# Last scatter behind the branch, three steps' sums and the first turned rows on VectorE, one gather earlier

## The chip, the cores and the metric

The kernel runs on one core of one Trainium2 chip. The metric is the device time of one execution in microseconds; the lower, the better. The core has five engines: PE (TensorE: matrix products), ACT (ScalarE), DVE (VectorE), POOL (GpSimd) and SP (SyncE, which here only issues DMAs). Each engine goes through its own instructions in order; semaphores hold an engine until another engine or a DMA is done. POOL issues the indirect DMAs (gathers and scatters by a list of row numbers).

## The reference

Two blocks follow each other. The first filters each of 8 sequences of 2496 rows and 256 channels in the frequency domain. The second sends each of the 19,968 resulting rows to the best of 8 experts, keeps the 80 rows with the largest gate of each expert, and runs those rows through the expert's two layers; all other rows of the output are zero.

```python
X = np.fft.rfft(x, axis=1)                       # x: 8 x 2496 x 256
y = np.fft.irfft(X * (filt_r + 1j*filt_i)[None], n=2496, axis=1)
x = y.reshape(8*2496, 256)
logits = x @ w_gate                              # 256 x 8
expert_idx = argmax(logits);  gate_w = softmax(logits)[expert_idx]
out = zeros((19968, 256))
for e in range(8):
    tok_idx = the rows with expert_idx == e, the 80 of largest gate_w
    h = np.maximum(x[tok_idx] @ w1[e], 0)        # 256 x 1024
    out[tok_idx] = gate_w[tok_idx, None] * (h @ w2[e])   # 1024 x 256
```

## The kernel before

**Spectra.** A sequence's transform of 2496 = 39 x 64 points is done as products with small tables. A loop over v = 0 to 81 walks through 80 steps (b, u): sequence b, part u of 10. In one turn of the loop stand: `stage2(b, u)`, which multiplies by a table into PSUM (`pb`, L334), takes the products with the filter's real and imaginary part on DVE (two instructions of 128x512, L342) and sums them on POOL (two of 128x256, L348: one subtraction and one addition); `transpose1` and `stage1` for later steps; and `turn` of the step two turns before, which turns the summed tile `p` by a product (`py`, L357), copies the spectrum out with ACT (`z` L372, `ysp` L373) and lets ACT send it to DRAM (`yf`, L376) every second step. SP loads `x` and writes zeros to the output (L193) from `zero_t`, a tile of zeros, at the same time. The order is written out by hand: each engine takes the instructions in the order in which the program gives them out.

**Rows.** Only the rows that an expert keeps are transformed back. From the logits a search finds the rows (`pick_...`, on DVE with small products on PE). For each sequence t, `fetch(t)` gathers the rows' table in two halves of 1280 columns from DRAM into `gts` (POOL, L476; 128 rows of 5 KB a half). `turn_rows(t, g)` turns four blocks of it by PE (`pw`, L493) and copies them to `wt` with ACT (L497); `add_rows(t, g)` multiplies them with four blocks of the sequence's spectrum (`po`, L504). After the fifth group ACT copies the result to `yr` (L509), and SP loads a further spectrum (`yb`, L484) and writes `yr` to `y_sel` in DRAM (L516). The groups of t = 0 to 2 stand in one list, those of t = 3 to 7 in another; `go(n)` gives out the next n entries, and the pieces of the search stand between. `turn_rows(0, 0)` and `turn_rows(0, 1)` stand right behind the last `turn`.

On POOL, the gathers for t = 0 and 1 stand between the last sums of the spectra (turns 76, 77 and 81 of the loop). Those for t = 3 to 5, the products `eval` for the search and the eight gathers of the gates (`gather_gates`, L225: 80 single numbers each) stand in this order:

```python
fetch(NE)              # NE = 3
pick_slots(1)
fetch(NE + 1)
...
pick_slots(2)          # idxs, idxt: the rows' numbers
gather_gates()
fetch(NE + 2)
```

`fetch(6)` and `fetch(7)` follow when the turned rows of t = 3 are given out. POOL's DMAs use eight semaphores in turn, and each waits until the one eight before it has landed.

**Experts.** For each expert the kept rows are gathered from `y_sel` (L1117), turned (`px`, `xs`), multiplied by w1 (`ph`, L1147), passed through relu (`hT`, by ACT and DVE) and multiplied by w2 (`po`, L1162). ACT multiplies by the gate (`ys`, L1165), and POOL scatters the 80 rows to the output (L1167). Expert 7 comes last.

**End.** A rare input (ties, an overfull list) needs a general path. Whether it does, the search has written to `bad`; behind the experts every engine reads this number (L1053) and branches (L1054). The input here doesn't need the path: every engine jumps to a short piece that brings the semaphores to the values which the general path would have left. On POOL this piece waits for all of POOL's DMAs and has an instruction INC_SWDGE_SEM for their semaphores. The program's end (L1566) follows: waits on SP, a DRAIN on POOL, and two barriers.

Of the kernel before, what the change touches and what calls it, by code (L numbers as in the profile page):

```python
# [11 lines left out]
AF = mybir.ActivationFunctionType  # L12
AX = mybir.AxisListType
F32 = mybir.dt.float32
BF16 = mybir.dt.bfloat16
I32 = mybir.dt.int32
# [7 lines left out]
B, S, C = 8, 2496, 256  # L24
N = B * S
N1, N2 = 39, 64
NS, NQ = 20, 64
NU = NS // 2
# [8 lines left out]
E, FF = 8, 1024  # L37
# [44 lines left out]
def kernel(  # L82
# [11 lines left out]
    nc = tc.nc  # L94
# [103 lines left out]

    idxs = consts.tile([cap, E], I32, name="idxs")
    idxg = consts.tile([cap, E], I32, name="idxg")  # L200
    gate = consts.tile([cap, E], F32, name="gate")
    idxt = consts.tile([cap, E], I32, name="idxt")
    idxb = consts.tile([128, B], I32, name="idxb")
# [30 lines left out]
    with ExitStack() as actx:  # L234
# [94 lines left out]
        def stage2(b, u):  # L329
            t2 = st.pop(("t2", b, u))  # L330
            ps = fps.tile([128, NDB, 2, 2, NQ], F32, name=f"pb_{b}_{u}", tag="f")
            for i in range(2):
                for cb in range(NDB):
                    nc.tensor.matmul(  # L334
                        out=ps[:, cb, i], rhs=d_t[:, 2 * u + i, :], start=True, stop=True,
                        lhsT=t2[:, i, 128 * cb:128 * cb + 128])
            pr = []
            for k in range(2):
                pt = ppool.tile([128, 2 * NDB, 2, NQ], F32, name=f"p{k}_{b}_{u}", tag=f"p{k}",
                                bufs=4 - 2 * k)  # L340
                f = ft[k][:, u].rearrange("p c s q -> p (c s) q")
                nc.vector.tensor_tensor(  # L342
                    out=pt, in0=ps[:].rearrange("p c s r q -> p (c s) r q"),
                    in1=f.unsqueeze(2).to_broadcast([128, 2 * NDB, 2, NQ]), op=AL.mult)
                pr.append(pt)
            yt = pr[0]
            for r, op in enumerate((AL.subtract, AL.add)):
                nc.gpsimd.tensor_tensor(out=yt[:, :, r, :], in0=yt[:, :, r, :],  # L348
                                        in1=pr[1][:, :, 1 - r, :], op=op)
            st["yt", b, u] = yt  # L350

        def turn(b, u):
# [136 lines left out]
        def turn_rows(t, g):  # L489
            ps = fps.tile([128, SG, 128], F32, name=f"pw_{t}_{g}", tag="f")  # L490
            for i in range(SG):
                s = SG * g + i
                nc.tensor.transpose(ps[:, i, :], gts[t // 2][:, t % 2, 128 * s:128 * s + 128],  # L493
                                    ident[:])
            if g % 2 == 0:
                wts[t, g // 2] = xpool.tile([128, 2, SG, 128], F32, name=f"wt_{t}_{g}", tag="x")
            nc.scalar.copy(out=wts[t, g // 2][:, g % 2], in_=ps[:])  # L497

        def add_rows(t, g):
            if g == 0:  # L500
# [233 lines left out]
        def pick_slots(part):  # L734
            f_t = st["f_t"]
            if part == 0:
                off_e = pt([128, 1], F32, "off_e", 1)
                nc.vector.tensor_copy(out=off_e[:], in_=st["poff"][:, 2, 0:1])
                slot = pt([128, KR], F32, "slot", 1)
                nc.vector.tensor_scalar(out=slot[:], in0=iota[:, 0:KR], scalar1=off_e[:, 0:1],  # L740
                                        scalar2=None, op0=AL.add)
                st["slot"] = slot
            elif part == 3:
                slot = st["slot"]
                st["eplc"] = xpool.tile([128, KR, cap], BF16, name="eplc", tag="x")
                nc.vector.tensor_tensor(
                    out=st["eplc"][:], in0=slot[:].unsqueeze(2).to_broadcast([128, KR, cap]),
                    in1=iota[:, 0:cap].unsqueeze(1).to_broadcast([128, KR, cap]),
                    op=AL.is_equal)
            elif part == 1:  # L750
                st["eval"] = pt([128, KR, 4, E], BF16, "eval_", 1)
                for i in range(4):
                    nc.gpsimd.tensor_tensor(
                        out=st["eval"][:, :, i, :],
                        in0=f_t[:, i, :].unsqueeze(2).to_broadcast([128, KR, E]),
                        in1=ehot[:].unsqueeze(1).to_broadcast([128, KR, E]), op=AL.mult)
            elif part == 2:
                pe = st["misc"][0:cap, 128:128 + 4 * E]
                for k in range(KR):
                    nc.tensor.matmul(pe, lhsT=st["eplc"][:, k, :],  # L760
                                     rhs=st["eval"][:, k].rearrange("p v e -> p (v e)"),
                                     start=(k == 0), stop=(k == KR - 1))
                es = st["es"] = pt([cap, 4, E], F32, "es", 1)
                nc.vector.tensor_copy(out=es[:].rearrange("p v e -> p (v e)"), in_=pe)
                nc.vector.scalar_tensor_tensor(out=idxg[:], in0=es[:, 1, :], scalar=128.0,
                                               in1=es[:, 0, :], op0=AL.mult, op1=AL.add)
                emp = pt([cap, E], F32, "emp", 1)
                nc.vector.tensor_scalar(out=emp[:], in0=es[:, 3, :], scalar1=st["off"][0:cap, 0:1],
                                        scalar2=float(N + S), op0=AL.is_le, op1=AL.mult)
                tokens(nc, sp, cap, es[:, 1, :], 0.0, es[:, 2, :], es[:, 3, :], -1.0, emp, idxs,  # L770
                       idxt)
            else:
                es = st["es"]
                inl = pt([cap, NO], F32, "inl", 1)
                nc.vector.tensor_scalar(out=inl[:], in0=es[:, 1, 0:NO], scalar1=float(B - 1),
                                        scalar2=None, op0=AL.is_equal)
                nc.vector.scalar_tensor_tensor(out=inl[:], in0=es[:, 0, 0:NO], scalar=1.0,
                                               in1=inl[:], op0=AL.add, op1=AL.mult)
                diag = fp.tile([cap, NO, cap], BF16, name="diag", bufs=1)
                nc.vector.tensor_tensor(  # L780
                    out=diag[:], in0=ident[0:cap, 0:cap].unsqueeze(1).to_broadcast([cap, NO, cap]),
                    in1=inl[:].unsqueeze(2).to_broadcast([cap, NO, cap]), op=AL.mult)
                last = st["last"] = fp.tile([128, NO, cap], F32, name="last", bufs=1)
                pd = st["misc"][:, 192:192 + NO * cap]
                nc.tensor.matmul(pd, lhsT=ones_bf[0:cap, :], start=True, stop=True,
                                 rhs=diag[:].rearrange("p e t -> p (e t)"))
                nc.vector.tensor_scalar(
                    out=last[:].rearrange("p e t -> p (e t)"), in0=pd, scalar1=pid[:, 0:1],
                    scalar2=1.0, op0=AL.subtract, op1=AL.is_equal)

        LATE, LEAD = 2, 2
        with tc.manual_schedule():
# [180 lines left out]
            fetch(NE)  # L973
            pick_slots(1)
            fetch(NE + 1)
            go(FG[5])
            pick_full(1, NE, B)
            pick_bad()
            go(next(i for i, w in enumerate(work) if w[1] == NE))
            pick_slots(2)  # L980
            gather_gates()
            fetch(NE + 2)
            go(8)
            pick_slots(4)
            go(next(i for i, w in enumerate(work) if w[:2] == ("m", B - 1)))
# [16 lines left out]
            for e in range(E):  # L1002
                if e + 3 < E:
                    ex.gather(e + 3)
                if e == 0:
                    ex.layer2(0)
                if e + 1 < E:
                    ex.layer1(e + 1)
                if e + 2 < E:
                    ex.turn(e + 2)  # L1010
                if e > 0:
                    ex.layer2(e)
                if e + 6 < E:
                    weights(e + 6, wpool, "w")

# [38 lines left out]
    with tc.If(n_bad > 0):  # L1054
# [22 lines left out]
        with (  # L1077
# [8 lines left out]
            for e in range(E):  # L1086
                load_weights(e, wp3.tile([128, 2 * NFC * C], F32, name=f"wg_{e}", tag="w"))
                ex.gather(e)
                ex.turn(e)
                ex.layer1(e)  # L1090
                ex.layer2(e)


class Experts:
# [59 lines left out]
                                scalar1=0.0, scalar2=None, op0=AL.max)  # L1154
        self.hT[e] = hT

    def layer2(self, e):
        nc, cap, nm = self.nc, self.cap, self.nm
        hT = self.hT.pop(e)
        po = self.bank(f"po{nm}_{e}")[:, 0:C]  # L1160
        for fc in range(NFC):
            nc.tensor.matmul(po[0:cap, :], lhsT=hT[:, fc, :], rhs=self.w2s[e][:, fc, :],  # L1162
                             start=(fc == 0), stop=(fc == NFC - 1))
        ys = self.fp.tile([cap, C], F32, name=f"ys{nm}_{e}", tag="ys")
        nc.scalar.activation(out=ys[:], in_=po[0:cap, :], func=AF.Copy,  # L1165
                             scale=self.gate[:, e:e + 1])
        nc.gpsimd.indirect_dma_start(  # L1167
            out=self.out[:, :],
            out_offset=bass.IndirectOffsetOnAxis(ap=self.idxs[:, e:e + 1], axis=0),
            in_=ys[:], in_offset=None, bounds_check=N - 1, oob_is_err=False)  # L1170


def tokens(nc, sp, cap, sq, sq0, bf, af, af0, emp, idxs, idxt):
# [397 lines left out]
```

## Time and profile before

| | |
|---|---|
| median of 17 runs | 476.37 us (473.71 to 481.25) |
| the profiled execution's own time | 476.19 us |
| its span, from first to last instruction | 474.4 us |
| mean granted TensorE clock | 0.981 |
| PE, ACT, DVE, POOL busy | 435.3, 222.7, 185.5, 183.8 us |
| DMA | 109.95 MB, 232 GB/s on average |

The span is that of the recorded instructions; the time also has 1.8 us around them. In the rows below, a group is given as line, engine, operation, tile written <- tiles read, partitions x elements, count; the bracket tells how long the engine was idle before it and what ended that. In the view of windows, each stretch has the busy time of PE, PEld (PE's loading of weights), DVE, ACT and POOL, then the granted clock, the DMA engines' share and GB/s. In the view of a line, the three numbers are the shortest, median and longest duration in ns, then the first and last start.

### The profile page before, as it was taken

What the parts mean: (1) busy time and instruction counts of PE and PEld (TensorE: products, weight loads), DVE (VectorE), ACT (ScalarE), POOL (GpSimd) and SP (SyncE); (2) the same over time, 40 slices, a digit from 0 to 9 for tenths busy, and PEclk for the clock granted to TensorE, in tenths of its full rate; (3) what the DMA queues carried; (4) which work ended last, traced back from release to release, by engine and by line L of the source; (5) the groups of instructions that cost most, each with busy time, mean ns of one, the idle gap of its engine ahead of it and who ended that gap; (6) DMA issues with size and microseconds to landing.
All of it is one profiled execution on the core that took longest, in us unless ns stands there. A gap on an engine that the chain in (4) does not pass through costs nothing. (4 is left out here: it accounts for less than half of the span.)

```text
span 474.4 us, 8669 instructions
## 1 busy us (share of the span) xinstructions
PE 435.3 (92%) x3380; PEld 409.9 (86%) x3380; DVE 185.5 (39%) x542; ACT 222.7 (47%) x364; POOL 183.8 (39%) x252
## 2 busy tenths in 40 slices
PE   4979999999999999999999997999939999999970
PEld 4869999999999999999999987888828888888850
DVE  2134554454664455655437984484200000110100
ACT  3846666666766666666667544322212231111110
POOL 7478344443543433543435548204550002113110
PEclk9999999999999999999999999999998999999995
DMA  7998367888777888778961326988857963999010
GB/s 205 264 264 261 127 196 238 244 259 250 262 237 250 270 274 250 208 267 267 386 263 68 121 103 205 356 311 305 310 178 287 368 223 91 376 388 301 8 28 2
DMA packets 39476, 109.95 MB, mean 232 GB/s; under 512 B 5073, under 2 KB 14608, under 8 KB 38658
## 3 DMA queue, kind: packets, MB, share of 16 engines
q1 hardware_dynamic: 28688, 76.41, 49.5%
q10 hardware_dynamic: 6178, 21.04, 11.3%
q0 software_dynamic: 4560, 11.86, 8.0%
q8 instruction: 29, 0.48, 0.4%
q14 instruction: 21, 0.17, 0.1%
HBM read 68.97 MB, written 43.20 MB: 236 GB/s over the span
## 5 line engine op out<-in xcount | busy, mean ns | idle before, releaser
L348 POOL TENSOR_TENSOR p<-p,p 128x256 f32<-128x256 f32 x160 | 114.0, 734 | 136.3 <-DVE p L342 107.9
L342 DVE TENSOR_TENSOR p<-pb,ft 128x512 f32<-128x512 f32 x160 | 102.2, 680 | 17.8 <-PE pb L334 11.3
L315 ACT COPY t<-pa 128x480 f32<-128x480 f32 x88 | 87.0, 1000 | 26.8 <-PE pa L309 26.2
L309 PE MATMUL pa<-wf_t,x 117*128 117x120 f32 x704 | 93.3, 281 | 6.1 <-DMA x<-in_x_dram 5.9
L309 PEld LDWEIGHTS pa<-wf_t,x 117*128 117x128 f32 x704 | 87.5, 198 | 6.2 <-DMA x<-in_x_dram 5.9
L357 PE MATMUL py<-gi,p 128*128 128x136 f32 x640 | 88.1, 280 | 2.3 <-POOL p L348 2.3
L334 PE MATMUL pb<-d_t,t 128*128 128x128 f32 x640 | 85.3, 276 | 2.3 <-remote 2.1
L357 PEld LDWEIGHTS py<-gi,p 128*128 128x128 f32 x640 | 79.8, 190 | 2.9 <-POOL p L348 2.9
L334 PEld LDWEIGHTS pb<-d_t,t 128*128 128x128 f32 x640 | 78.0, 191 | 3.3 <-remote 2.2
L325 ACT COPY t<-pt 128x512 f32<-128x512 f32 x80 | 46.8, 585 | 66.6 <-PE pt L323 60.0
L504 PE MATMUL po<-yb,wt 128*128 128x256 f32 x240 | 58.8, 390 | 8.4 <-ACT wt L497 8.4
L504 PEld LDWEIGHTS po<-yb,wt 128*128 128x128 f32 x240 | 44.7, 196 | 14.3 <-ACT wt L497 9.1
L497 ACT COPY wt<-pw 128x512 f32<-128x512 f32 x40 | 23.1, 586 | 53.4 <-PE pw L493 42.0
L323 PE MATMUL pt<-ident,t 128*128 128x128 f32 x320 | 48.0, 273 | 0.0
L379 DVE COPY z<-py 128x16 f32<-128x16 f32 x60 | 11.2, 186 | 92.0 <-ACT ysp L373 57.9
L323 PEld LDWEIGHTS pt<-ident,t 128*128 128x128 f32 x320 | 37.6, 142 | 0.0
L373 ACT COPY ysp<-py 128x512 f32<-128x512 f32 x60 | 35.4, 590 | 0.0
L1147 PEld LDWEIGHTS ph<-xs,w 128*128 128x128 f32 x256 | 29.7, 192 | 1.7 <-DVE xs L1138 1.1
L1147 PE MATMUL ph<-xs,w 128*128 128x80 f32 x256 | 29.8, 274 | 0.8 <-DVE xs L1138 0.8
L1162 PE MATMUL po<-w,hT 128*80 128x256 f32 x128 | 28.8, 379 | 0.0
L1117 POOL DMA_INDIRECT xg<-y_sel,idxg x8 | 7.7, 962 | 47.5 <-DMA y_sel<-yr 45.6
L1167 POOL DMA_INDIRECT out_dram<-ys,idxs x8 | 7.5, 932 | 46.1 <-ACT ys L1165 46.1
(195 smaller groups left out, 331.8 us busy)
## 6 DMA issues: line engine op xcount, KB each, us to landing
out_dram<-zero_t SPq DMA_DIRECT2D x64, 312.0 KB
x<-in_x_dram SPq DMA_DIRECT2D x40, 468.0 KB
w<-in_moe_w_dram SPq DMA_DIRECT2D x16, 1024.0 KB
yf<-ysp ACTq DMA_DIRECT2D x30, 512.0 KB
yb<-yf SPq DMA_DIRECT2D x6, 2560.0 KB
yf<-ys ACTq DMA_DIRECT2D x10, 512.0 KB
x<-in_x_dram SPq DMA_DIRECT2D x8, 234.0 KB
d_t<-d_tbl SPq DMA_DIRECT2D x5, 256.0 KB
```

Source lines behind the costliest of these rows:

```text
L309: nc.tensor.matmul(out=ps[:, i, :, 2 * NS * cb:2 * NS * cb + 2 * NS], lhsT=xt[0:NJ * N1, (2 * k + i) % JC, 128 * cb:128 * cb + 128], rhs=w ...
L315: nc.scalar.copy(out=t1[:, 2 * k - h:2 * k - h + 2], in_=ps[:])
L323: nc.tensor.transpose(ps[:, i, cb, :], t1[:, a:a + 2, :].rearrange("p r n -> p (r n)"), ident[:])
L325: nc.scalar.copy(out=t2[:].rearrange("p i c -> p (i c)"), in_=ps[:].rearrange("p i c q -> p (i c q)"))
L334: nc.tensor.matmul(out=ps[:, cb, i], rhs=d_t[:, 2 * u + i, :], start=True, stop=True, lhsT=t2[:, i, 128 * cb:128 * cb + 128])
L342: nc.vector.tensor_tensor(out=pt, in0=ps[:].rearrange("p c s r q -> p (c s) r q"), in1=f.unsqueeze(2).to_broadcast([128, 2 * NDB, 2, NQ]), ...
L348: nc.gpsimd.tensor_tensor(out=yt[:, :, r, :], in0=yt[:, :, r, :], in1=pr[1][:, :, 1 - r, :], op=op)
L357: nc.tensor.matmul(out=ps[:, i, ZW * cb:ZW * cb + ZW], rhs=gi[:, cb, :], lhsT=yt[:, 2 * cb + i].rearrange("p r q -> p (r q)"), start=True, ...
L373: nc.scalar.copy(out=dst.rearrange("p s (h w) -> p s h w", h=2), in_=pv[:, :, :, 0:128])
L504: nc.tensor.matmul(pos[t][:, 0, 0:C], lhsT=wts[t, g // 2][:, g % 2, i, :], rhs=ybs[t][:, s, :], start=(s == 0), stop=(s == NS - 1))
L1147: nc.tensor.matmul(ph[:, fc // 4, fc % 4, 0:cap], lhsT=self.w1s[e][:, k, 128 * fc:128 * fc + 128], rhs=xs[:, k, :], start=(k == 0), stop=( ...
L1162: nc.tensor.matmul(po[0:cap, :], lhsT=hT[:, fc, :], rhs=self.w2s[e][:, fc, :], start=(fc == 0), stop=(fc == NFC - 1))
```

## The change

The program changes in four places, and nothing of what is computed does.

1. `stage2`: in the last three steps, (7, 7), (7, 8) and (7, 9), DVE does the two sums of the filter's products; in the others POOL still does.
2. `turn_rows`: DVE copies the first turned rows (t = 0, g = 0); ACT copies the others.
3. `fetch(NE + 2)` stands right behind `fetch(NE + 1)`, ahead of `gather_gates`.
4. Expert 7's result goes into a part of `zero_t` instead of a tile of the pool, and its scatter is given out behind the `if` of the general path, with a copy of its row numbers in a tile of its own (`idx_last`, by DVE). POOL's branch then stands behind the scatter of expert 6. The piece behind the `if` is a new one, from which every engine goes on to the program's end by one more jump.

```diff
+    idx_last = consts.tile([cap, 1], I32, name="idx_last")
+    ys_last = zero_t[0:cap, 0:C]
...
             for r, op in enumerate((AL.subtract, AL.add)):
-                nc.gpsimd.tensor_tensor(out=yt[:, :, r, :], in0=yt[:, :, r, :],
-                                        in1=pr[1][:, :, 1 - r, :], op=op)
+                adder = nc.gpsimd if (b, u) < (B - 1, NU - 3) else nc.vector
+                adder.tensor_tensor(out=yt[:, :, r, :], in0=yt[:, :, r, :],
+                                    in1=pr[1][:, :, 1 - r, :], op=op)
...
-            nc.scalar.copy(out=wts[t, g // 2][:, g % 2], in_=ps[:])
+            copy = nc.vector.tensor_copy if (t, g) == (0, 0) else nc.scalar.copy
+            copy(out=wts[t, g // 2][:, g % 2], in_=ps[:])
...
+                nc.vector.tensor_copy(out=idx_last[:], in_=idxs[:, E - 1:E])
...
             fetch(NE + 1)
+            fetch(NE + 2)
...
             gather_gates()
-            fetch(NE + 2)
...
-                    ex.layer2(e)
+                    ex.layer2(e, keep=ys_last if e == E - 1 else None)
...
+    scatter(nc, out, ys_last, idx_last[:])
...
-    def layer2(self, e):
+    def layer2(self, e, keep=None):
...
-        ys = self.fp.tile([cap, C], F32, name=f"ys{nm}_{e}", tag="ys")
-        nc.scalar.activation(out=ys[:], in_=po[0:cap, :], func=AF.Copy,
+        ys = keep
+        if keep is None:
+            ys = self.fp.tile([cap, C], F32, name=f"ys{nm}_{e}", tag="ys")[:]
+        nc.scalar.activation(out=ys, in_=po[0:cap, :], func=AF.Copy,
                              scale=self.gate[:, e:e + 1])
-        nc.gpsimd.indirect_dma_start(
-            out=self.out[:, :],
-            out_offset=bass.IndirectOffsetOnAxis(ap=self.idxs[:, e:e + 1], axis=0),
-            in_=ys[:], in_offset=None, bounds_check=N - 1, oob_is_err=False)
+        if keep is None:
+            scatter(nc, self.out, ys, self.idxs[:, e:e + 1])
+
+
+def scatter(nc, out, ys, idx):
+    nc.gpsimd.indirect_dma_start(
+        out=out[:, :], out_offset=bass.IndirectOffsetOnAxis(ap=idx, axis=0), in_=ys,
+        in_offset=None, bounds_check=N - 1, oob_is_err=False)
```

## The prediction

> **What bounds the kernel now.** I read the busy shares first, then the windows by stage, then the waits and the timeline where TensorE (PE) has holes, and last the rows behind the final matmul.
>
> ```profile
> PE 435.3 (92%) x3380; PEld 409.9 (86%) x3380; DVE 185.5 (39%) x542; ACT 222.7 (47%) x364; POOL 183.8 (39%) x252
> 340.00:350.00 10.00, 7.23 (x42) 6.21 (x40) 0.47 (x1) 1.17 (x2) 7.76 (x8) 1.00 0.41 132
> 350.00:360.00 10.00, 4.67 (x16) 3.62 (x14) 0.00 (x0) 1.45 (x3) 1.99 (x2) 0.68 0.88 314
> ```
>
> PE is the bound: 435.3 of 474.4 us. A gain must fill one of its holes or shorten the end. There are three: small ones at 292 to 296 us, a large one at 340 to 360 (PE busy 11.9 of 20, granted clock 0.68 in its second half), and 14.9 us behind the last matmul (459.5).
>
> Hole 1, from the timeline:
>
> ```profile
> 290.72 2.77 POOL L348 TENSOR_TENSOR p<-p,p 128x256 f32<-128x256 f32 x4
> 292.19 1.19 PE L357 MATMUL py<-gi,p 128*128 128x136 f32 x8 [1.38 <-POOL p L348]
> 294.57 1.04 PE L493 MATMUL pw<-ident,gts 128*128 128x128 f32 x8
> 295.85 1.07 ACT L497 COPY wt<-pw 128x512 f32<-128x512 f32 x2 [0.40 <-issue]
> 296.49 1.99 PE L504 MATMUL po<-ys,wt 128*128 128x256 f32 x8 [0.88 <-ACT wt L497]
> ```
>
> PE waits 1.38 us for POOL's last sums (1.42 us a step, between gathers of 1.0 us), then 0.88 us for ACT's copy of the turned rows.
>
> Hole 2, from the waits of 294 to 360 us:
>
> ```profile
> PE po L504 <- ACT wt L497: 9.3, 4, 5.3
> ACT yr L509 <- remote: 6.4, 1, 6.4
> ACT wt L497 <- remote: 6.3, 2, 5.9
> ```
>
> PE stood 2.77 us before 347.8 and 5.33 before 355.56, waiting for ACT, and ACT for something the profile can't name ("remote"). It falls into the time in which POOL issues the eight gate gathers (334.9 to 344.7) and six row gathers (345.0 to 352.5). Next the clock halves: the L504 group of 8 at 355.56 took 3.78 us against 1.99, the next groups 0.65 more. Together 2.77 + 5.33 + 1.79 + 0.65 = 10.5 us.
>
> Hole 3, the rows of the branch (L1054) and of the program's end (L1566) after 460 us:
>
> ```profile
> L1054 POOLq EVENT_SEMAPHORE  x5: 17/43/43, 463.4 to 466.2; - x5
> L1054 POOLq COMPARE_BRANCH  x1: 53/53/53, 460.7 to 460.7; - x1
> L1054 POOLq INC_SWDGE_SEM  x1: 1556/1556/1556, 466.3 to 466.3; - x1
> L1566 POOLq DRAIN  x3: 46/103/5623, 467.9 to 474.1; - x3
> L1566 SPq DRAIN  x3: 7/7/13, 468.6 to 473.8; - x3
> ```
>
> POOL alone sets the end: scatter at 460.32, branch at 460.67, first instruction of the path not taken at 463.4 (2.8 us later), the second at 466.0 (a hole of 2.5 us with nothing to wait for), then the 1.56 us INC_SWDGE_SEM and a DRAIN of 5.62 us to 473.5, and 0.85 us of barriers. SP was through at 468.6.
>
> **The change part by part.** All in the times of this execution (476.19 us, span 474.4; the median of the runs is 476.37, so 0.2 above it).
>
> *Sums of the last three steps by VectorE (DVE).* Six additions of 128x256 leave POOL (6 x 0.73 us) and join DVE. No row has just this; L535 (128x256, two SBUF inputs) took 0.42, so a step costs DVE 0.84 more. DVE's products end at 287.35 for the first; with the additions between, the steps end at 288.2, 290.3 and 292.4 (each: products 1.27 + 0.84, PE's pb being there). The last was ready at 293.49 on POOL, so the last turn starts near 292.45 instead of 293.54: -1.1 us. DVE has nothing else but 0.4 us until 301. POOL's four row gathers now follow each other: 287.0, 288.3, 289.6, 290.9 instead of 287.0, 289.7, 293.6, 295.0. They are wanted after 293, so earlier gains nothing itself.
>
> A rule speaks against this. POOL's L348 pair at 281.10 took 2.17 us instead of 1.42 beside two-input DVE work:
>
> ```profile
> 281.10 2.17 POOL L348 TENSOR_TENSOR p<-p,p 128x256 f32<-128x256 f32 x2 [2.77 <-DVE p L342]
> ```
>
> The Trainium skill, "SBUF — State Buffer", section "Who interferes with whom", has it that a DVE instruction with two SBUF inputs and a GpSimd instruction that reads SBUF shut each other out. By the rule each gather may be held by a pair of additions (0.84 us), so the fourth ends 2.5 us later than I say, still before 295. By the row, a 0.75 us stretch at most. The first gather starts before any addition and landed at 292.9, before PE wants it at 293.4. So 0 either way; if that landing slipped past 293.4, the excess would come straight off the 1.1.
>
> *First turned rows by DVE.* ACT at 293 to 295 has z, ysp and a DMA issue ahead of the copies. DVE reads PSUM at 0.29 us for 128x128 (L512) and 0.48 for 128x312 (L406), so 128x512 costs 0.69. Turned rows start at 293.45, their first group ends near 294.0, DVE is through at 294.7, and PE's L504 starts at 294.75 instead of 296.49. ACT's second copy comes at 294.8, while PE wants it 4 us later. Both parts: -1.7 us (0 to -2.2). From there to 342 PE has no hole over 0.9 us, so the lead is kept.
>
> *One gather ahead of the gates.* Two issues (1.0 us each, 1.3 apart) move from behind the eight gate gathers to before them. The gates wait for idxt of DVE in any case (334.9), so their start costs nothing. The eight semaphores of POOL's DMAs go round, so the last two gates now wait for the moved gather to land, in competition with SP's spectrum load (332 to 342). The gates are read only from 408, so 60 us cover this; SP's spectrum, which the moved gather may hold back by 3 us, landed at 342 and is multiplied first after 357. The remaining four row gathers start some 2.6 us earlier. Whether hole 2 shrinks I can't derive, since its cause isn't named. Bounds: nothing left of it (-10.5); longer by the time the moved gather needs in the crowded stretch (1.3 MB at the 0.4 MB/us of 336 to 342: +3.3). I take half of the two issues, -1.3: its second wait ended when the row gathers were through, and there are a third fewer of them.
>
> *Last scatter behind the branch.* POOL no longer waits for the last ys before it branches. The scatter before starts at 456.86, and branch follows 0.35 later: 457.2; path not taken at 460.0. The 2.5 us hole lies at a fixed place of POOL's program (between its 708th and 709th instruction). POOL's program is 11 instructions shorter there, so the hole moves 11 instructions on, right in front of the scatter: INC_SWDGE_SEM runs 460.3 to 461.9 under it, and the scatter starts at 462.7 (its ys is ready at 460.0). It ends at 463.6; then DRAIN 5.62 and barriers 0.85: 470.1 instead of 474.4, so -4.3 us. SP must see the landing (2.1 to 2.7 us after the start by the trace of the last scatter: 465.4) and is through by 466.3, so it is hidden by DRAIN.
>
> What DRAIN waits for no row shows. If it hangs on INC_SWDGE_SEM and lets the scatter pass, the end is 468.5 (-5.9). If it hangs on it and blocks the scatter, 471.9 (-2.5); if it then comes a second time, 475.0 (+0.6). If the hole still lies ahead of INC_SWDGE_SEM, 2.5 us are lost in each. I take -4.3: the row that stands between.
>
> A second rule: each engine gets a further jump to the end. The skill, "Runtime: NRT & Kernel Launch", section "Instruction fetch mechanics", says that a taken branch to code not yet fetched stalls until it is. The taken branch here cost 2.8 us; a second such stall would leave -1.5. But the jump from the path not taken to the end exists already, and DVE went through it from 456.7 to its DRAIN at 456.8: 0.1 us, to neighbouring code. I count nothing.
>
> One DVE copy of idx_last (0.16 us by L1191, with 5 us of slack before L785) and the same ACT write into another tile: 0. The zero writes that read this tile ended long before.
>
> **Sum:** -1.7 - 1.3 - 4.3 = -7.3 us, 468.9 against 476.19, so 469.1 for the median.
>
> **The rivals.**
> *The hole closes* (0.13): fewer gathers behind the gates, no halved clock: -1.7 - 10.5 - 4.3, so 460. For it: the wait ends with the gathers; against: the gates, which may be its cause, stay.
> *The end doesn't gain* (0.22): INC_SWDGE_SEM's work blocks the scatter and hole 2 stays: -1.7 and -2.5 to +0.6, so 472.2 to 475.3.
> *Slower* (0.15): the scatter becomes serial with POOL's closing work. Hole ahead of INC_SWDGE_SEM (464.4), its 5.62 us blocks the scatter until 470.1, then 0.91 and DRAIN again: 477.6, +3.2; with the lead +1.5, 477.9. It decides from a scatter start of 470.1 on (470.1 + 0.91 + 5.62 + 0.85 = 477.5, against 474.4 + 1.7 of lead). For it: the scatter does move behind two steps of unknown cause; against: the branch is taken 3.5 us earlier. A longer hole 2 would end on the same side.
>
> **How the numbers follow.** Main case 0.50: 469.1, own range 466 to 472. About 0.3% (1.4 us) can be told from no change. Faster: 0.50 + 0.13 + most of the 0.22 = 0.77; same 0.09; slower 0.14. The range 461.5 to 477 leaves out half of "closes" and half of "slower".
>
> **What would show it.** Right: last L348 on DVE with PE's first L504 near 294.7; POOL's COMPARE_BRANCH before the last ys; INC_SWDGE_SEM straight after the first event; scatter at 461 (462.7 less the lead) and no row of 2.5 us ahead of it. Wrong: PE's hole at 345 to 355 much shorter or longer; a DRAIN of 5.6 us ahead of the scatter or after it twice; L504 still released by ACT or by the gather.

## The result, and the profile after

The changed kernel takes 463.0 us (median of 8 runs, 461.9 to 465.1) against 476.55 (47 runs): ratio 0.9713, 95% interval 0.9689 to 0.9738, faster by 13.5 us. The profiled executions agree: spans of 460.9 and 474.4 us. The forecast was 469.1. Its direction and its range held; the size did not come from where the sum had it.

The span divides at three points that both traces have: PE's first product with turned rows (`po<-ys`), PE's first product for the experts (`px`), and the end of the last `ys`. Worked out from the starts in the two traces:

| part of the span, us | before | after | difference | forecast |
|---|---|---|---|---|
| start to first `po<-ys` | 296.49 | 294.89 | -1.6 | -1.7 |
| first `po<-ys` to first `px` (rows) | 101.80 | 93.92 | -7.9 | -1.3 |
| first `px` to end of last `ys` (experts) | 61.76 | 61.71 | 0 | 0 |
| end of last `ys` to end of span | 14.34 | 10.35 | -4.0 | -4.3 |

So two of the three terms came out within 0.3 us, and the middle one, which the prediction said it couldn't derive, is six times its size. Executions differ by some 4 us in how soon they come to the last steps of the spectra, whatever the edits. So the front is better counted from PE's third last product into `pb` (284.66 and 284.77 us): from there to the first `po<-ys` it is 11.83 us before and 10.12 after, -1.7; in every run below it is 11.8 without edits 1 and 2 and 10.1 with them.

The front, from the timeline after (start, length, then the instruction group; the bracket is the idle time before it and what ended it):

```profile
291.12 0.99 POOL L479 DMA_INDIRECT gts<-rows_tbl,idxb  x1 [0.31 <-issue]
291.51 0.76 DVE L351 TENSOR_TENSOR p<-p,p 128x256 f32<-128x256 f32 x2
292.42 1.16 PE L360 MATMUL py<-gi,p 128*128 128x136 f32 x8 [0.58 <-issue]
293.42 1.04 PE L496 MATMUL pw<-ident,gts 128*128 128x128 f32 x8
294.06 0.69 DVE L501 COPY wt<-pw 128x512 f32<-128x512 f32 x1 [1.65 <-PE pw L496]
294.89 1.97 PE L508 MATMUL po<-ys,wt 128*128 128x256 f32 x8 [0.44 <-DVE wt L501]
```

A pair of sums takes DVE 0.76 us (0.84 had been worked out), the first turned rows 0.69 (0.69), and PE waits 0.58 and 0.44 us where it waited 1.38 and 0.88.

The middle, from the windows after (columns as in the prediction: PE, PEld, DVE, ACT, POOL, then clock, DMA share, GB/s), with the three rows of the timeline that explain the first window:

```profile
330.00:340.00 10.00, 8.32 (x52) 6.96 (x51) 2.58 (x16) 2.21 (x5) 5.68 (x8) 0.83 0.96 366
340.00:350.00 10.00, 10.00 (x56) 8.72 (x55) 0.47 (x1) 3.13 (x6) 6.40 (x7) 1.00 0.50 180
350.00:360.00 10.00, 10.00 (x57) 8.82 (x57) 0.27 (x1) 3.09 (x6) 1.28 (x2) 1.00 0.90 365
```

```profile
330.17 0.75 PE L764 MATMUL misc<-eval__1_3660,eplc 128*80 128x32 bf16 x16
332.77 0.19 DVE L768 COPY es<-misc 80x32 f32<-80x32 f32 x1 [5.71 <-PE pw L496]
333.52 3.67 PE L508 MATMUL po<-yb,wt 128*128 128x256 f32 x8 [1.68 <-ACT wt L501]
```

PE is busy through 340 to 360, where it was busy for 11.9 of 20 us. A smaller stall is new at 331.8: the product into `misc` ended at 330.9, but DVE's copy of it starts only at 332.8, some 1.8 us late; PE then stands 1.68 us, and the next group of 8 takes 3.67 us instead of 1.99, at half the clock. Idle and slow time together are some 3.5 us, against 10.5 before. The stall before begins in the same way, with a product and ACT's copy of it:

```profile
342.26 0.60 PE L493 MATMUL pw<-ident,gts 128*128 128x128 f32 x4
347.16 0.58 ACT L497 COPY wt<-pw 128x512 f32<-128x512 f32 x1 [5.91 <-remote]
```

The product ends at 342.86 in the record, and the copy follows 4.30 us later, where in e7 below such a copy follows within 0.1 us as a rule and 0.4 at most, if ACT is free. Below, this is called a late semaphore of PE. The ends of PE's records are modelled, so it may also be that the product itself ended later than the record says.

The end, from the rows of the branch (L1059), the last scatter (L1180) and the program's end (L1578): shortest, median and longest duration in ns, then first and last start.

```profile
L1059 POOLq EVENT_SEMAPHORE  x5: 17/43/43, 450.3 to 450.7; - x5
L1059 POOLq COMPARE_BRANCH  x1: 53/53/53, 447.7 to 447.7; - x1
L1059 POOLq INC_SWDGE_SEM  x1: 1540/1540/1540, 450.8 to 450.8; - x1
L1180 POOL DMA_INDIRECT out_dram<-zero_t,idx_last x1: 912/912/912, 453.5 to 453.5; - x1
L1578 POOLq DRAIN  x3: 46/109/6443, 453.6 to 460.6; - x3
```

POOL branches at 447.7, 2.8 us ahead of the end of the last `ys` (450.53). The five events of the path now lie within 0.4 us (2.8 before); the scatter starts at 453.49, and the DRAIN ends at 460.03, 5.63 us behind the scatter's end. There is one DRAIN of this kind, not two.

### The profile page after: what moved, and what is told of

Same layout as the page of the kernel before. It is cut to its first block, busy times and chain, and to the rows that moved or that the text cites. A ratio compares the mean times of both kernels' runs of the same rounds, so it can differ in the third digit from the quotient of the medians.

```text
span 460.9 us, 8667 instructions
## 1 busy us (share of the span) xinstructions
PE 433.8 (94%) x3380; PEld 409.2 (89%) x3380; DVE 188.4 (41%) x550; ACT 222.5 (48%) x363; POOL 179.9 (39%) x246
## 5 line engine op out<-in xcount | busy, mean ns | idle before, releaser
L351 POOL TENSOR_TENSOR p<-p,p 128x256 f32<-128x256 f32 x154 | 110.0, 736 | 136.3 <-DVE p L344 88.8
L344 DVE TENSOR_TENSOR p<-pb,ft 128x512 f32<-128x512 f32 x160 | 102.1, 680 | 17.4 <-PE pb L336 10.9
L311 PE MATMUL pa<-wf_t,x 117*128 117x120 f32 x704 | 92.2, 278 | 7.1 <-DMA x<-in_x_dram 6.9
L311 PEld LDWEIGHTS pa<-wf_t,x 117*128 117x128 f32 x704 | 86.2, 195 | 7.5 <-DMA x<-in_x_dram 6.0
L1168 PEld LDWEIGHTS po<-w,hT 128*80 128x80 f32 x128 | 18.6, 150 | 7.5
L479 POOL DMA_INDIRECT gts<-rows_tbl,idxb x16 | 16.1, 1009 | 21.0 <-DVE idxb L695 16.7
```

What stands on the lines that cost most here:

```text
L311: nc.tensor.matmul(out=ps[:, i, :, 2 * NS * cb:2 * NS * cb + 2 * NS], lhsT=xt[0:NJ * N1, (2 * k + i) % JC, 128 * cb:128 * cb + 128], rhs=w ...
L344: nc.vector.tensor_tensor(out=pt, in0=ps[:].rearrange("p c s r q -> p (c s) r q"), in1=f.unsqueeze(2).to_broadcast([128, 2 * NDB, 2, NQ]), ...
L351: adder.tensor_tensor(out=yt[:, :, r, :], in0=yt[:, :, r, :], in1=pr[1][:, :, 1 - r, :], op=op)
```

## The experiments

Twelve runs were made, each beside the kernel before on the same chip. They fell on four chips, and these differ: on the first (e1 to e4) the kernel before takes 476.3 us, as in the comparison above, on the second (e5 to e8) 465.7, on the third (e9, e10) 466.2 and on the fourth (e11, e12) 466.4. Each ratio is against the kernel before on the same chip. The table has the parts of each profiled execution, as above. The kernel before has a profile on the first chip alone; on the others its time is known, and how it runs there is read from e7, which differs from it by three short instructions.

| kernel | median, us | before there | ratio (95%) | rows | last `ys` to end |
|---|---|---|---|---|---|
| e1 gather only | 467.8 | 476.3 | 0.9821 (0.9797 to 0.9845) | 93.7 | 14.08 |
| e2 gather back | 469.3 | 476.3 | 0.9874 (0.9833 to 0.9916) | 99.0 | 10.65 |
| e3 end only | 475.6 | 476.3 | 0.9971 (0.9941 to 1.0001) | 102.1 | 13.12 |
| e4 front only | 471.4 | 476.3 | 0.9914 (0.9887 to 0.9941) | 100.4 | 12.31 |
| e5 no gates | 460.7 | 465.7 | 0.9881 (0.9845 to 0.9916) | 90.8 | 11.10 |
| e6 gates last | 459.4 | 465.7 | 0.9880 (0.9821 to 0.9939) | 91.1 | 10.74 |
| e7 three more | 463.4 | 465.7 | 0.9947 (0.9915 to 0.9978) | 92.7 | 12.08 |
| e8 gather held | 459.9 | 465.7 | 0.9880 (0.9826 to 0.9933) | 90.8 | 10.72 |
| e9 changed kernel | 459.3 | 466.2 | 0.9834 (0.9785 to 0.9882) | 90.8 | 10.70 |
| e10 gates last, four fewer | 459.1 | 466.2 | 0.9858 (0.9820 to 0.9895) | 91.1 | 10.47 |
| e11 no gates | 462.3 | 466.4 | 0.9914 (0.9888 to 0.9941) | 90.8 | 11.05 |
| e12 gather only | 463.9 | 466.4 | 0.9950 (0.9924 to 0.9976) | 90.8 | 14.14 |

The part of the experts took 61.7 to 61.8 us in every one of them.

**e1 and e2: is it the gather?** The edit in e1, made on the kernel before; e2 undoes just this in the changed kernel:

```diff
             fetch(NE + 1)
+            fetch(NE + 2)
...
             gather_gates()
-            fetch(NE + 2)
```

> The kernel before with edit 3 alone: the gather of t = 5 stands ahead of the gates' gathers; the sums, the first turned rows and the last scatter stay as they were. Theory A (the row gathers that stand behind the gates cause the large hole at 340 to 360): two gathers less behind the gates take most of it away, by itself -8 us (468.5 against 476.5), and the profile shows PE's clock at half speed for less than 4 us instead of 6.8, and no wait of ACT for "remote" in 335 to 360. Rival B (the hole went because everything came 1.7 us earlier, or by the clock gate's phase): within 1 us of the kernel before. Rival C (the prediction's own -1.3): 475.

> The changed kernel with edit 3 alone undone: the gather of t = 5 stands behind the gates again; the other three edits stay. Theory A: the hole comes back, with two waits of ACT for "remote" behind 335 us: 8 us longer than the changed kernel, 471. Rival B (the lead of 1.7 us did it): as fast as the changed kernel, 463. Rival C: 464.5.

e1 took 467.8 us, -8.5, and e2 469.3, +6.3 on the changed kernel's 463.0 (by the ratios, +7.7). The rows take 93.7 us in e1, as in the changed kernel, and 99.0 in e2, where the kernel before has 101.8. The two stalls of the kernel before, that of e1, and those of e2:

```profile
347.80 1.99 PE L504 MATMUL po<-yb,wt 128*128 128x256 f32 x8 [2.77 <-ACT wt L497]
355.56 3.78 PE L504 MATMUL po<-yb,wt 128*128 128x256 f32 x8 [5.33 <-ACT wt L497]
```

```profile
335.34 3.45 PE L504 MATMUL po<-yb,wt 128*128 128x256 f32 x8 [1.59 <-ACT wt L497]
```

```profile
349.20 3.24 PE L508 MATMUL po<-yb,wt 128*128 128x256 f32 x8 [4.28 <-issue]
354.88 1.99 PE L508 MATMUL po<-yb,wt 128*128 128x256 f32 x8 [1.59 <-ACT wt L501]
```

In e1 this is PE's one hole of the stage; in e2 there are two again, 4.28 and 1.59 us long, with two waits of ACT for "remote" of 7.4 and 3.6 us. So the gather's place is what shrank the hole on this chip. The lead of the front is not: e1 has none, and e4 below has it and keeps both stalls.

**e3 and e4: which edit shortens the end?** e3 has the last scatter behind the branch and nothing else, e4 the sums and the turned rows on DVE and nothing else. The edits are those of the change's diff.

> The kernel before with edit 4 alone: expert 7's scatter is given out behind the branch. What the profiles of before and after show (14.35 us from the last ys to the span's end before, 10.35 after) belongs to this edit alone: -4.0 us, 472.5 against 476.5; the last ys to the span's end 10.3 to 10.5 us, INC_SWDGE_SEM straight behind the first event of the path, one DRAIN of 5.6 us behind the scatter. Rival: the lead of the earlier edits changes how far POOL is ahead of the last ys, so that alone the edit brings only the hidden branch or less: -2.5 or less.

> The kernel before with edits 1 and 2 alone: the last three steps' sums and the first turned rows by VectorE. The profiles of before and after have PE's first L504 product 1.6 us earlier, and nothing behind it that should eat this: -1.7 us, 474.8 against 476.5, with the large hole at 338 to 358 as large as before (10.5 us). Rival B (the large hole hangs on the lead): it shrinks with these edits alone, -5 us or more.

Both missed, in opposite directions: e3 -1.4 us by its ratio (0 to -2.8) instead of -4.0, e4 -4.1 instead of -1.7. In e4 the stalls of the rows are there with the lead, 2.41 and 3.64 us of idle time, each followed by a slow group:

```profile
345.64 3.42 PE L506 MATMUL po<-yb,wt 128*128 128x256 f32 x8 [2.41 <-issue]
353.39 3.41 PE L506 MATMUL po<-yb,wt 128*128 128x256 f32 x8 [3.64 <-ACT wt L499]
```

By the parts, what e3 is short of lies at the end; of what e4 has beyond its forecast, 2.0 us lie at the end and 1.4 in the rows (100.4 us against 101.8). The rows of POOL's branch, in e3 and then in e4:

```profile
L1059 POOLq EVENT_SEMAPHORE  x5: 17/43/43, 460.6 to 463.3; - x5
L1059 POOLq INC_SWDGE_SEM  x1: 1540/1540/1540, 463.4 to 463.4; - x1
```

```profile
L1056 POOLq EVENT_SEMAPHORE  x5: 17/43/43, 460.4 to 460.8; - x5
L1056 POOLq INC_SWDGE_SEM  x1: 1556/1556/1556, 460.9 to 460.9; - x1
```

In e3 the five events still spread over 2.7 us: the hole of 2.5 us is there, now between the third and the fourth event, two instructions further on than before. In e4 the events lie within 0.4 us: the hole has left the path, though e4 doesn't touch the end. It is the six sums that left POOL, with their waits, that moved it: POOL's records up to the branch are nine fewer in e4 than before. A gap of 0.35 us is left, in front of POOL's semaphore clear (0.03 us before), nine records further on than the hole. From the last `ys` to the end, e4 has 12.31 us instead of 14.34 (-2.0), and e2, which has edits 1, 2 and 4, 10.65 (-1.7 more). So the 4.0 us of the change are about half the position of POOL's program, given by the sums' edit, and half the hidden branch.

**e7: is the hole a position?** The kernel before with three instructions more at POOL's start:

```diff
+    pad = consts.tile([1, 4], F32, name="pad")
+    for i in range(3):
+        nc.gpsimd.memset(pad[:], 0.0)
     idxs = consts.tile([cap, E], I32, name="idxs")
```

> The kernel before with three more instructions on POOL, memsets of four numbers, at the start of the program; nothing else. They take 0.1 us each at a time when POOL is idle. If the hole of 2.5 us behind the first event of the path not taken belongs to a place in POOL's instructions (a border that the program crosses), three more instructions push that border out of the path, to ahead of its first event: path not taken 2.6 to 2.9 us behind the branch, the second event 0.1 us behind the first, and 2.4 us faster than before, 474.0 against 476.4. Rival (the hole is a wait for something else, or is bound to the event): no change, 476.4.

```profile
L1057 POOLq EVENT_SEMAPHORE  x5: 17/43/43, 453.1 to 453.4; - x5
L1057 POOLq COMPARE_BRANCH  x1: 53/53/53, 450.1 to 450.1; - x1
```

463.4 us against 465.7, -2.3 (-2.5 by the ratio): as expected of a position, and more work made the kernel faster. The first event still comes 3.0 us behind the branch.

The place can be counted in POOL's records from the start of each trace. Without edit 4 it is always behind the 407th: there stand the holes of the kernel before, e1 and e12 (2.53, 2.39 and 2.20 us), and there stands e4's gap of 0.35 us; in e7 it falls ahead of the branch, while POOL waits for `ys`. With edit 4 it is behind the 406th: there stands e3's hole (2.44 us); in e6 and e8 it falls right in front of the last scatter, which starts 1.13 us behind the last event instead of 0.78, and in e10 behind the long DRAIN, where a gap of 0.39 us stands. (e5 and e11 have fewer records than that.) So the same place costs 2.2 to 2.5 us just behind a branch's target and some 0.35 us where POOL reaches it later.

e7 also shows the rows' stage of the kernel before on a chip where PE's semaphores aren't late. Its timeline, and the window of 346 to 354 us in e7 and then in the profile of before:

```profile
353.51 0.63 PE L496 MATMUL pw<-ident,gts 128*128 128x128 f32 x4 [1.73 <-DMA gts<-rows_tbl,idxb]
```

```profile
346.00:354.00 8.00, 6.27 (x36) 5.29 (x35) 0.00 (x0) 1.57 (x3) 3.91 (x4) 1.00 0.95 380
```

```profile
346.00:354.00 8.00, 2.43 (x12) 1.94 (x12) 0.00 (x0) 0.58 (x1) 4.96 (x5) 0.97 0.67 186
```

There is no half clock and no "remote". What is left of the hole has a name: PE waits 1.73 us for the gather of t = 5 itself, given out at 343.3 behind the gates. The clock stays full behind this wait; behind one of 1.68 us in the profile of after it was halved, so how long PE stands in the record doesn't tell alone what the clock does.

In the window of 346 to 354 us the DMA engines move 380 GB/s in e7 and 186 in the profile of before. By queue (packets, MB, share of the 16 engines; q0 is POOL's, the gathers), before and then in e7:

```profile
q0 software_dynamic: 566, 1.49, 66.7%
```

```profile
q1 hardware_dynamic: 253, 2.14, 64.8%
q0 software_dynamic: 426, 0.90, 29.9%
```

So the gathers move no less in the profile of before. The other 2.14 MB in e7 are almost all the next spectrum. SP gives it out at the moment at which ACT copies `yr`, when PE's last product with an earlier spectrum is seen to be done, and in the profile of before that is late as well. The load there, then in e7:

```profile
354.17 0.32 SPq L484 DMA_DIRECT2D yb<-yf  x1
```

```profile
343.15 0.32 SPq L487 DMA_DIRECT2D yb<-yf  x1
```

**e5 and e11: are the gates the cause?** The kernel before without the eight gathers of `gather_gates`:

```diff
         nc.gpsimd.memset(gate[:], 0.0)
-        for e in range(E):
-            nc.gpsimd.indirect_dma_start(
-                out=gate[:, e:e + 1], out_offset=None, in_=gates_dram[:, :],
...
```

> The kernel before without the eight gathers of the gates (the gates stay zero, so the rows are multiplied by zero): its row gathers for t = 5 to 7 follow those of t = 4 directly or wait only for their tile. Theory A1 (the gates' gathers and the row gathers right behind them together cause the large hole at 340 to 360): the hole goes, 465 to 468.5, as with edit 3 alone or better, and what is left of PE's waits lies ahead of 336. Rival A2 (the gates have no part in it, six row gathers in a row hold PE up, wherever they stand): within 2 us of the kernel before, 474.5 to 478, with two waits of ACT for "remote" of over 4 us each.

> The kernel before without the gates' eight gathers once more (the gates stay zero, so the rows are multiplied by zero), since the first time fell on a chip where the kernel before shows no late semaphores. Where the kernel before takes about 476: if the gates' gathers are what makes PE's semaphores come late, the hole at 340 to 360 goes, 475.9 - 10.5 - 0.8 for the shorter end: 464 to 465.5; if it is the row gathers, 475. Where it takes about 466: as before, ratio 0.988.

Both fell on chips where nothing points to late semaphores in the kernel before (465.7 and 466.4 us), so neither answers the question of the first chip. They gave -5.1 and -4.1 us. By the parts of e5, the rows are 1.9 us shorter than in e7, since the gather of t = 5 is early, and the end is 1.0 us shorter than in e7. The latter was new:

```profile
L1049 POOLq INC_SWDGE_SEM  x1: 1396/1396/1396, 450.2 to 450.2; - x1
L1561 POOLq DRAIN  x3: 46/103/4970, 451.6 to 457.2; - x3
```

INC_SWDGE_SEM took 1.40 instead of 1.56 us and the DRAIN 4.97 instead of 5.62, with 60 DMAs given out by POOL instead of 68. e10 follows this up.

**e6 and e8: the gates elsewhere, the gather held.** In e6 `gather_gates()` of the changed kernel stands behind `fetch(7)`; in e8 `fetch(NE + 2)` stands right ahead of the gates and waits for their row numbers:

```diff
+            held = consts.tile([cap, E], I32, name="held")
+            nc.gpsimd.tensor_copy(out=held[:], in_=idxt[:])
+            fetch(NE + 2)
             gather_gates()
```

> The changed kernel with the gates' gathers behind all row gathers (behind the one of t = 7) instead of ahead of those of t = 6 and 7. The gates are read only from 395 on. Theory A1: nothing stands behind the gates any more, so no late semaphore of PE at 336 to 346; the smaller stall at 331.8 to 333.5 with its half clock (3.5 us) lies ahead of the gates and stays: 462 to 463 against 463. Rival A3 (the small stall comes from the gates' semaphores too): 459.5. Rival A4 (the gates hold up whatever runs beside them, now the rows of t = 5 and 6): 466 or more.

> The changed kernel with the gather of t = 5 held until the rows' numbers (idxt) are there, by a copy of idxt on POOL in front of it; it still stands ahead of the gates. POOL then gives out two row gathers at 327 to 329.3, two more at about 333, and the gates from 335.5 on. If the small stall of the changed kernel at 331.8 to 333.5 (PE's semaphore comes 1.8 us late while POOL gives out the third and fourth row gather) comes from four row gathers in a row, it goes, with the half clock after it: -3.5 us, 459.5 against 463. Rival (the stall only moves with the gathers): 462 to 464, with a late semaphore at 335 to 338. Second rival (row gathers next to the gates are what makes the large hole): it comes back in part, 466 or more.

459.4 and 459.9 us, both ratio 0.988, on a chip without late semaphores: the rows take 91.1 and 90.8 us, as in e9 (below) without these edits. They show only that the gates' place is free, and that giving out the gather of t = 5 at 333.1, over 3 us later, costs nothing. Whether they would take away the small stall of the first chip stays open.

**e9 and e10: the changed kernel on such a chip, and fewer DMAs from POOL.** e10 is e6 with four loads given out by SP:

```diff
-            nc.gpsimd.dma_start(out=gi[:, 0, 128:128 + E], in_=moe_w_gate[0:128, :])
+            nc.sync.dma_start(out=gi[:, 0, 128:128 + E], in_=moe_w_gate[0:128, :])
...
```

> The changed kernel as it is, beside the kernel before, on whichever chip this falls. The runs so far fell on two: on one the kernel before took 476.3 us, with late semaphores of PE at 340 to 354; on the other 465.7, without them. Where the kernel before takes about 476: ratio 0.971 as in the first comparison, 463. Where it takes about 466 (no late semaphores): the front (1.7), the hole at POOL's border (2.4), the branch (1.6) and at most the 1.7 us that PE waited there for the gather of t = 5: 458.5 to 460, ratio 0.985 to 0.988. If the ratio there is 0.971 too, the late semaphores are not what edit 3 takes away.

> The changed kernel with the gates' gathers behind those of all rows, and with four loads at the start (gi twice, e_t, wi_t) given out by SP instead of POOL. Without the gates' eight gathers INC_SWDGE_SEM took 1.40 us instead of 1.56 and the DRAIN 4.97 instead of 5.62: 0.020 and 0.082 us for each DMA that POOL gives out in the whole program (68 before). If that is a price for each, four fewer give 1.46 and 5.29 us behind the scatter's end, 0.4 us off the end; if both hang on the gates' gathers themselves (their 4-byte rows), they stay at 1.54 and 5.62. The gates at the end: where the semaphores of PE come late, 459 to 460 if the gates are their cause, 463 or more if the row gathers are; where they don't, within 1 us of the changed kernel beside it, less the 0.4.

The changed kernel takes 459.3 us there against 466.2: ratio 0.9834, -7.7 us by the ratio and -6.9 by the medians. Over 40% of what it brings on the first chip is gone, and the prediction's sum (-7.3) fits. In e9 DVE's copy of `misc` follows the product's start by 0.80 us (2.60 in the profile of after), and PE has no hole over 0.3 us in the stage:

```profile
330.35 0.19 DVE L768 COPY es<-misc 80x32 f32<-80x32 f32 x1 [3.91 <-PE misc L764]
```

e10's end, with 64 DMAs of POOL:

```profile
L1059 POOLq INC_SWDGE_SEM  x1: 1460/1460/1460, 445.5 to 445.5; - x1
L1578 POOLq DRAIN  x3: 50/253/6440, 447.9 to 455.4; - x3
```

INC_SWDGE_SEM is 80 ns shorter than the changed kernel's 1540. The DRAIN begins ahead of the scatter's record and ends 5.31 us behind the scatter's end (5.63 in e9). Expected were 1.46 and 5.29. The time, 459.1, can't be told from e9's; from the end of the DRAIN to the end of the span e10 needs 1.31 us and e9 0.85, since the place in POOL's program now lies there.

**e12: what edit 3 is worth without late semaphores.**

> The kernel before with edit 3 alone once more. Where the kernel before takes about 476: ratio 0.982 as the first time. Where it takes about 466: what is left for edit 3 is PE's wait for the gather of t = 5 near 353 us (1.73 us in the profile of the kernel with three more instructions), -1.7, 464.4, ratio 0.996; if edit 3 is worth as much there as on the first chip (-8.5), late semaphores are not what it takes away.

463.9 us against 466.4, -2.3 by the ratio (1.1 to 3.5), where the same kernel brought -8.5 on the first chip. Its rows take 90.75 us against 92.7 in e7, so 1.9 us, and PE's wait for the gather near 353 is gone. So some 2 us of edit 3 are the gather's own lateness, and the other 6 were found only where PE's semaphores come late.

## Why the prediction was right, and where it was not

- *Sums on DVE and first turned rows*: right, -1.7 for -1.7. The first, third and fourth gather ran beside a pair of sums and took 1.08, 1.02 and 0.99 us, the second beside none 1.02, so the sums did not hold them up. The rule weighed there was applied to the wrong work: the same section (the Trainium skill, "SBUF — State Buffer", "Who interferes with whom") says further on that `tensor_copy` was seen to stall DMAs but `tensor_tensor`, which these sums are, was not, and this trace agrees. POOL's own sums are another case, as the row of 2.17 us showed. The step left out that taking six sums off POOL also shortens POOL's program. That gain was booked under the scatter.
- *"The 2.5 us hole lies at a fixed place of POOL's program ... so the hole moves 11 instructions on"*: right as a mechanism, shown by e3 (two instructions on), e4 (nine on, out of the path) and e7 (pushed back out of it). That it moves "right in front of the scatter" is one record off: by the count it lies behind the scatter's, and no loss shows there. The gap of 0.78 us in front of the scatter has nothing to do with it, since e3, whose hole is elsewhere, has it too; what it is stays open. So the forecast of the scatter's start, 2.66 us behind the last `ys` for 2.96 measured, came out near in part by luck: it let the hole set this start, and POOL's own steps do. The Trainium skill, "Runtime: NRT & Kernel Launch", section "Instruction fetch mechanics", has instructions streamed in blocks, in sequence, with the crossing of a border mostly hidden and a branch breaking the sequence. That fits a border that costs 2.5 us only where it stands right behind a branch's target. The trace of before has two packets of 8 KB in a queue of kind "instruction" that start inside the hole (463.67 and 464.36 us); e7 has two behind its first event as well, without a hole, and no record says which engine they are for. So a wait for the fetch fits, and it is not shown.
- *The last scatter behind the branch*: -4.3 forecast, -4.0 measured. The case taken (DRAIN once, 5.6 us behind the scatter's end) is what the profile shows; the cases of -5.9, -2.5 and +0.6 are out. Of the 4.0, e4 gives 2.0 to the shorter program, so edit 4, on top of the others, is worth 1.7 to 2.0 (by e3, alone, 1.2 to 1.4). The second jump cost nothing that shows.
- *"One gather ahead of the gates ... I take half of the two issues, -1.3"*: this is the term that was mis-sized; it measured -7.9. Two things were missed. PE needs the gather of t = 5 near 353 us and would wait for it in any case: 1.7 to 1.9 us, which e7's row names and which the profile of before hides under the longer stall. And on the first chip the stall depends on the gather's place: in the rows' part e1 and e2 show 8.1 and 5.1 us for it, in the medians 8.5 and 6.3. That the whole came out near the range's low end and inside it owes something to luck: on the third chip the same edits bring -7.7.
- *"From there to 342 PE has no hole over 0.9 us, so the lead is kept"*: true of the trace it was read from, not of the changed kernel on that chip. Part of the stall came back at 331.8, where four row gathers now follow each other: 1.68 us idle and some 1.8 lost to the half clock.
- The result lies between the main case (466 to 472) and the rival "The hole closes" (460), and outside the main case's own range. The chance of 0.13 for that rival was too low, given that the bound of -10.5 stood in the sum with no reason against it.

What makes PE's semaphores come late on the first chip is not settled. The runs show that it goes with the place of the row gathers, and that it needs more than this program: no run on the three other chips has it. Whether it is the chip itself or its state at that time, no run tells, since no later one fell on it. A wait of PE for its own instructions is unlikely: in the profile of before no packet of a queue of kind "instruction" lies between 342.6 and 378 us. The six traces of that chip also tell the landing of no DMA at all, where the eight others tell 44 to 68 each, so their semaphore events are not complete, and "remote" may mean no more than that; PE's and ACT's idle time stands in the records of their instructions. e5, e6, e8, e10 and e11 were to part the gates from the row gathers there, and none of them met that chip.

## What to carry to other kernels

A gather that stands behind others on its queue is late by all of their issues; ask for each of them when it is first read, and put those that are read last (here the gates, over 50 us ahead of their use) behind those that are read next. Behind the last product, POOL's own instructions are the path here: how many stand before a branch was worth over 2 us, and each DMA that POOL had given out 0.1 us. Where a stall has no named releaser, its whole length belongs in the range, and the comparison wants a second chip.

## What the runs showed of the hardware

- POOL's closing work grows with the DMAs that it has given out in the whole program: DRAIN 5.62, 5.31 and 4.97 us for 68, 64 and 60 (before, e10, e5; in e10 counted from the scatter's end), so 0.082 us each, and INC_SWDGE_SEM 1.56 us with 68 DMAs ahead of it, 1.54 with 67, 1.46 with 63 and 1.40 with 60 (before, after, e10, e5), so 0.020 us each. Eight gathers cost 0.8 us at the end, beside their issue.
- A border in POOL's program just behind a branch's target costs 2.2 to 2.5 us (before, e1, e3, e12) on top of the 2.6 to 3.0 of the branch; the same border elsewhere costs some 0.35 us (e4, e6, e8). Nine records fewer (e4) or three more (e7) take it off the path.
- On one chip of four, the copies of PE's products came late though the records have the products at their ends: 1.8 us (`misc`) in the profile of after, 4.3 us in that of before (at most 0.4 us on the other chips). In the rows' stage this chip is behind the others by 9.1 us with the kernel before (101.8 against 92.7) and by 3.1 with the changed one (93.9 against 90.8).
